# Windowed attention and a three-product MoE: queries, keys and values laid out by token and chunk, with an order of its own

## The chip, the cores and the metric

The kernel runs on one core of one Trainium2 chip. The metric is the device time of one execution in microseconds, the median of several; preparing the inputs on the host is not part of it. The engines are named as in the profile: PE is TensorE (PEld its weight loads), DVE VectorE, ACT ScalarE, POOL GpSimd, SP SyncE; SPq and ACTq are the two queues on which transfers are issued.

## The reference

Attention over 8 batches of 8 heads with 64 elements each: 512 local tokens look at the 32 global ones and at the local ones within 32 positions, and the 32 global tokens look at all 544. The 544 x 8 result rows of 512 elements (4352 rows) go through an MLP with a gate that is 0 below -1, h above 1 and a parabola between:

```python
k_all = np.concatenate([k_g, k_l], axis=2)
v_all = np.concatenate([v_g, v_l], axis=2)
out_g = np.matmul(sm(scale * np.matmul(q_g, k_all.transpose(0, 1, 3, 2))), v_all)
s_ll = np.where(np.abs(pos[:, None] - pos[None, :]) <= 32, scale * np.matmul(q_l, k_l.transpose(0, 1, 3, 2)), -1e9)
s_lg = scale * np.matmul(q_l, k_g.transpose(0, 1, 3, 2))
out_l = np.matmul(sm(np.concatenate([s_lg, s_ll], axis=-1)), v_all)
x = np.concatenate([out_g, out_l], axis=2).transpose(0, 2, 1, 3).reshape(B * S, H * D)
h = x @ w_in
g = np.where(h >= 1, h, np.where(h <= -1, 0.0, (h + 1) ** 2 / 4))
return (g @ w_out).astype(np.float32)
```

Queries, keys, values and the result are float32. The two weights, 512 x 2048 and 2048 x 512, come as float64, so 8 MB each.

## The kernel before, in words

Every number is carried as two float16 halves with a scale, and each product is made of three matrix products (high x high, high x low, low x high). The work is written as named steps.

**Weights.** 16 tiles of w_in (`load_win`, two transfers of 256 KB each, in rows of 1 KB) and 16 of w_out (two transfers of 256 KB, rows of 2 KB) are decoded from float64 words by integer operations, mostly on VectorE (`win_decode`, `wout_decode`), squared on TensorE for a scale, and split into halves.

**A batch.** `load` fetches queries, keys and values (lines 551 to 583). Tokens go to partitions, so a tile is 128 tokens x 8 heads x 64 elements. Queries: four tiles of 128 tokens and one of the 32 global ones. Keys and values: six tiles ("chunks"); the first five hold the 32 global tokens and 96 local ones, the last 32 global, 32 local and 32 global. In memory q_l is batch, head, token, element, so what one partition receives is eight pieces of 64 floats. A chunk takes two transfers (global and local part), the last one three: 13 transfers for the keys of a batch, 13 for the values, 5 for the queries. `scale_q`, `scale_k` and `scale_v` find a scale for each; for batch 0 the scales of queries and keys come from Gram products of the raw tiles on TensorE (`gram`, line 585; 24 products for the keys of six tiles), for the others from squares on ScalarE. `prep_q`, `prep_k` and `prep_v` split a tile in halves; queries and keys are then transposed, in batch 0 by TensorE with a copy from PSUM by ScalarE or VectorE, later by DMA transposes on SP's queue. `swap_q` and `prep_w` copy between on-chip tiles by transfers of 2 KB runs. `att_q` to `att_x` do the local attention, `glob_a` and `glob_b` the global one, `moe_f` and `moe2` the MLP of 256 tokens at a time (`moe1` for the first two).

**Order.** The steps are first recorded in order of a planned time and cut into segments (line 98), a run of calls on one engine; each transfer is a segment of its own. `ORDER` (line 1293) lists the segments' numbers in the order in which they are issued. TensorE, VectorE, ScalarE and GpSimd execute them exactly in that order; transfers are kept in the listed order within the queues that issue them, so a transfer on ScalarE's queue stands behind the ScalarE instructions ahead of it in the list. `SLOTS` gives each tile its place. `T["queues"]` says of each plain transfer whether SP's (s) or ScalarE's (a) queue issues it; a load on SP's queue waits until the load five before it there has landed (`AHEAD`, line 1342). Other letters of `T` choose the engine of an operation: `casts` and `subs` for the high and low half of the softmax, `turns` for the copy after a transposition, `glow`, `lows` and `lowx` for low halves in the MLP (v is VectorE, a ScalarE, p GpSimd). Since all instructions are replayed from one place, they have one line in the profile, L1365, plain transfers L1368 and DMA transposes L1370; groups are told apart by tiles.

Of the kernel before, what the change touches and what calls it, by code (L numbers as in the profile page):

```python
# [131 lines left out]
def attention_moe(nc, memory, q_l, k_l, v_l, q_g, k_g, v_g, w_in, w_out, out):  # L132
    B, H, S, D = q_l.shape
    SG = q_g.shape[2]
    DM, DFF = w_in.shape
    P = 128
# [4 lines left out]
    NTOK = SG + S  # L141
# [69 lines left out]
    def load_dma(o, i):  # L211
        nc.sync.load(o, i)
# [338 lines left out]
    def load_kv(src_l, src_g, b, nm, part):  # L551

        got = []
        for c in (2 * part, 2 * part + 1):
            if c == NC - 1:
                st = st4.tile([P, H, D], F32, tag="st4", name=f"{nm}{b}_{c}")
                for o in (0, 2 * QB):
                    load_dma(st[o:o + QB], src_g[b].rearrange("h p d -> p h d"))
                load_dma(st[QB:2 * QB], src_l[b][:, S - QB:S, :].rearrange("h p d -> p h d"))
                got.append((st, 3 * QB))  # L560
                continue
            st = stg.tile([P, H, D], F32, tag="st", name=f"{nm}{b}_{c}")
            load_dma(st[0:QB], src_g[b].rearrange("h p d -> p h d"))
            load_dma(st[QB:P], src_l[b][:, 96 * c:96 * c + 96, :].rearrange("h p d -> p h d"))
            got.append((st, P))
        return got

    def load_q(b, part):
        c = 2 * part
        if c == NI:  # L570
            st = st4.tile([P, H, D], F32, tag="st4", name=f"qg{b}")
            load_dma(st[0:SG], q_g[b].rearrange("h p d -> p h d"))
            return [(st, SG)]
        got = []
        for u in range(2):
            st = stg.tile([P, H, D], F32, tag="st", name=f"q{b}_{c + u}")
            load_dma(st, q_l[b][:, (c + u) * P:(c + u + 1) * P, :].rearrange("h p d -> p h d"))
            got.append((st, P))
        return got

    def load(b, nm, part):
        r = load_q(b, part) if nm == "q" else load_kv(*{"k": (k_l, k_g), "v": (v_l, v_g)}[nm], b, nm, part)
        BT[b].setdefault("raw" + nm, {}).update({2 * part + u: x for u, x in enumerate(r)})
# [710 lines left out]

SLOTS = {
# [49 lines left out]
def build(tc, *args):  # L1345
# [4 lines left out]
    with ExitStack() as ctx:  # L1350
# [10 lines left out]
        with tc.manual_schedule(engines={E.PE, E.DVE, E.Activation, E.Pool}):  # L1361
            for n in order:
                for engine, op, a, k in again[n]:
# [13 lines left out]
                    moved.append(r)  # L1377


_INS = ["q_l", "k_l", "v_l", "q_g", "k_g", "v_g", "moe_w_in", "moe_w_out"]  # L1380
_OUTS = [((4352, 512), "float32")]


# [23 lines left out]
```

## Time and profile before

| | |
|---|---|
| median of 3 runs | 893.72 us (892.99 to 897.49) |
| the profiled execution, its own time | 897.37 us |
| its span in the profile | 895.6 us |
| mean granted TensorE clock, of full speed | 0.991 |
| TensorE busy | 841.7 us (94%) |
| VectorE busy | 716.7 us (80%) |
| ScalarE busy | 645.8 us (72%) |
| GpSimd busy | 348.0 us (39%) |
| moved by transfers | 140.97 MB in 379,713 packets |

The span is from the first to the last instruction; the execution's own time has some 2 us around it. Busy shares are of the span, and say nothing of which engine a stage waits for; that is read from stretches and waits. The DMA share of a stretch can exceed 1.

### The profile page before, as it was taken

Reading aid. Unit: us, or ns where it says so; the run is one execution under the profiler, and the core shown is the slowest. Engines: PE = TensorE matmul, PEld = TensorE weight load, DVE = VectorE, ACT = ScalarE, POOL = GpSimd, SP = SyncE. Lnnn points to the kernel's source line nnn. Section 1 sums busy time; section 2 is a strip of 40 time slices with the busy share of each in tenths; the row PEclk is TensorE's granted clock in tenths of the full one; section 3 lists DMA queues with packets and bytes.
Section 4 is the critical chain, followed back from the end, with each engine's and each line's share of the span. In section 5 each row is a group of like instructions: output and inputs, shape, how many; then the busy total and the mean of one; then the engine's idle time right before and its main releaser. Section 6 shows DMA issues by size and latency. Waiting matters only on the chain.

```text
span 895.6 us, 35249 instructions
## 1 busy us (share of the span) xinstructions
PE 841.7 (94%) x14398; PEld 613.1 (68%) x14398; DVE 716.7 (80%) x1967; ACT 645.8 (72%) x1632; POOL 348.0 (39%) x545
## 2 busy tenths in 40 slices
PE   1667999999999999899999999999999999999998
PEld 1534899557876766867585967767676867588743
DVE  3998999997878997787878888788988988757741
ACT  2489998888787976785888767876888578455530
POOL 4236457725333244332346235323214233315160
PEclk9988999999999999999999999999999999999999
DMA  9998798599988999998997899999998974584001
GB/s 228 251 234 216 201 196 139 121 189 191 172 143 176 166 181 177 169 156 173 177 181 141 173 155 172 182 166 142 189 173 163 176 135 97 113 142 82 2 1 59
DMA packets 379713, 140.97 MB, mean 157 GB/s; under 512 B 348576, under 2 KB 357792, under 8 KB 379552
## 3 DMA queue, kind: packets, MB, share of 16 engines
q1 hardware_dynamic: 314864, 102.28, 66.6%
q10 hardware_dynamic: 64688, 36.45, 18.8%
q8 instruction: 112, 1.84, 0.9%
q14 instruction: 49, 0.40, 0.2%
HBM read 49.81 MB, written 8.91 MB: 66 GB/s over the span
## 4 chain that ended last, share of the span: by engine, by line
PE 69%; DMA 4%; DVE 4%; ACT 2%; issue 1%; SPq 0%; ACTq 0%; DVEq 0%
PE bank L1365 69%; DMA room<-room 3%; DVE room L1365 3%; ACT room L1365 2%; DMA keys_kt<-room 1%; DVE bank L1365 1%; DMA room<-in_v_g_dram 1%; ACTq L1368 0%; SPq L1368 0%; SPq L1370 0%; DVE weights_w L1365 0%; DVE small_nb L1365 0%; DVE batch_small_ms L1365 0%; DVE small_gs L1365 0%; DVE twin L1365 0%
## 5 line engine op out<-in xcount | busy, mean ns | idle before, releaser
L1365 POOL TENSOR_TENSOR room<-room,room 128x256 f16<-128x256 f32 (+4 forms) x408 | 278.5, 708 | 452.0 <-ACT room L1365 366.3
L1365 PEld LDWEIGHTS <-room 128*32 128x32 f16 (+3 forms) x7576 | 251.4, 97 | 235.9 <-issue 25.1
L1365 PE MATMUL bank<-weights_w,room 128*128 128x512 f16 x1632 | 366.4, 379 | 1.6 <-DVE room L1365 1.3
L1365 PEld LDWEIGHTS <-weights_w 128*128 128x128 f16 (+1 forms) x3968 | 220.2, 98 | 20.0 <-issue 6.8
L1365 PE MATMUL bank<-room,weights_w 128*128 128x128 f16 (+1 forms) x3840 | 220.4, 216 | 3.8 <-issue 3.0
L1365 ACT CAST room<-room 128x512 f16<-128x512 f32 (+1 forms) x245 | 140.1, 587 | 61.4 <-DVE room L1365 34.3
L1365 PE MATMUL bank<-room,twin 128*128 128x128 f16 (+1 forms) x2304 | 129.0, 216 | 0.5 <-ACT room L1365 0.5
L1365 PEld LDWEIGHTS <-twin 128*128 128x128 f16 x2304 | 123.6, 98 | 3.8 <-issue 0.6
L1365 ACT ACTIVATE room<-room,small_nb 128x128 f32<-128x128 f32 x256 | 100.8, 395 | 10.9 <-DVE small_nb L1365 9.0
L1365 ACT ACTIVATE room<-bank,batch_small_ms 128x512 f32<-128x512 f32 (+1 forms) x112 | 83.1, 750 | 31.9 <-DVE bank L1365 9.8
L1365 DVE SCALAR_TENSOR_TENSOR bank<-bank,batch_small_ms,room 128x512 f32<-128x512 f32 (+1 forms) x112 | 80.4, 723 | 12.6 <-ACT room L1365 12.4
L1365 ACT COPY room<-bank 128x512 f32<-128x512 f32 (+2 forms) x107 | 63.1, 596 | 33.0 <-PE bank L1365 18.0
L1365 ACT ACTIVATE junk_junka<-room 128x512 f16<-128x512 f32 (+2 forms) x120 | 74.9, 624 | 11.9 <-DMA room<-in_q_l_dram 3.1
L1365 DVE SCALAR_TENSOR_TENSOR room<-room,batch_small_ms,bank 128x512 f32<-128x512 f32 (+1 forms) x112 | 78.9, 711 | 1.2
L1365 DVE CUSTOM_DVE_ANT_0 room<-bank,const_mask,batch_small_q 128x128 f32<-128x128 f32 x256 | 73.7, 345 | 6.3 <-PE bank L1365 5.5
L1365 DVE TENSOR_TENSOR room<-room,room 128x512 f16<-128x512 f32 (+1 forms) x89 | 63.9, 724 | 17.5 <-ACT room L1365 16.4
L1365 DVE TENSOR_TENSOR bank<-bank,room 128x512 f32<-128x512 f32 (+1 forms) x64 | 41.5, 658 | 20.5 <-PE bank L1365 20.3
L1365 DVE SCALAR_TENSOR_TENSOR room<-room,batch_small_ms,room 128x512 f32<-128x512 f32 (+1 forms) x64 | 48.5, 760 | 3.0 <-ACT room L1365 2.6
L1365 DVE TENSOR_SCALAR room<-bank,batch_small_ms 128x512 f32<-128x512 f32 x34 | 25.1, 743 | 31.5 <-PE bank L1365 29.0
L1365 ACT ACTIVATION_READ_ACCUMULATOR room<-room,small_nb 128x1 f32 x256 | 48.8, 191 | 0.0
L1365 DVE SCALAR_TENSOR_TENSOR room<-room,batch_small_sv,room 128x512 f16<-128x512 f32 (+1 forms) x47 | 38.2, 818 | 5.6 <-ACT room L1365 5.1
L1365 DVE SCALAR_TENSOR_TENSOR room<-room,batch_small_sk,room 128x512 f16<-128x512 f32 (+1 forms) x46 | 35.7, 788 | 7.4 <-ACT room L1365 7.4
(174 smaller groups left out, 886.3 us busy)
## 6 DMA issues: line engine op xcount, KB each, us to landing
room<-room SPq DMA_DIRECT2D x75, 128.0 KB, 3.7
room<-room ACTq DMA_DIRECT2D x69, 128.0 KB, 3.7
twin<-in_moe_w_out_dram SPq DMA_DIRECT2D x22, 256.0 KB, 4.9
room<-in_q_l_dram SPq DMA_DIRECT2D x21, 256.0 KB, 5.1
room<-in_v_l_dram SPq DMA_DIRECT2D x28, 192.0 KB, 3.7
room<-in_k_l_dram SPq DMA_DIRECT2D x24, 192.0 KB, 4.2
weights_w<-in_moe_w_in_dram ACTq DMA_DIRECT2D x17, 256.0 KB, 4.5
out_dram<-room SPq DMA_DIRECT2D x17, 256.0 KB, 2.6
```

The source lines that it names most:

```text
L1365: getattr(getattr(tc.nc, engine), op)(*a, **k)
```

## The change

The host arranges the inputs: `q_all` is batch, token, head, element, local tokens first and then the global ones; `k_all` and `v_all` hold the six chunks of a batch one after another, 736 tokens, with the global tokens repeated in each chunk. A tile is then one transfer, 2 KB contiguous per partition. A batch's keys take 6 transfers instead of 13, its values 6 instead of 13, its queries 5 as before: 464 plain transfers in all instead of 576, with the same bytes.

```diff
-            if c == NC - 1:
-                st = st4.tile([P, H, D], F32, tag="st4", name=f"{nm}{b}_{c}")
-                for o in (0, 2 * QB):
-                    load_dma(st[o:o + QB], src_g[b].rearrange("h p d -> p h d"))
-                load_dma(st[QB:2 * QB], src_l[b][:, S - QB:S, :].rearrange("h p d -> p h d"))
-                got.append((st, 3 * QB))
-                continue
-            st = stg.tile([P, H, D], F32, tag="st", name=f"{nm}{b}_{c}")
-            load_dma(st[0:QB], src_g[b].rearrange("h p d -> p h d"))
-            load_dma(st[QB:P], src_l[b][:, 96 * c:96 * c + 96, :].rearrange("h p d -> p h d"))
-            got.append((st, P))
+            tail = c == NC - 1
+            n = 3 * QB if tail else P
+            st = (st4 if tail else stg).tile([P, H, D], F32, tag="st4" if tail else "st", name=f"{nm}{b}_{c}")
+            load_dma(st[:n], src[b, c * P:c * P + n])
+            got.append((st, n))
...
-            load_dma(st, q_l[b][:, (c + u) * P:(c + u + 1) * P, :].rearrange("h p d -> p h d"))
+            load_dma(st, q_all[b, (c + u) * P:(c + u + 1) * P])
...
+    def rows(*parts):
+        return _np.concatenate(parts, axis=2).transpose(0, 2, 1, 3)
+
+    def chunks(g, x):
+        return rows(*[y for c in range(0, 480, 96) for y in (g, x[:, :, c:c + 96])], g, x[:, :, 480:512], g)
+
+    laid["q_all"] = rows(inputs["q_l"], inputs["q_g"])
+    laid["k_all"] = chunks(inputs["k_g"], inputs["k_l"])
+    laid["v_all"] = chunks(inputs["v_g"], inputs["v_l"])
```

With it come a new `ORDER`, new `SLOTS`, new `queues` and new letters. Apart from the loads the segments are the same ones, so the old and the new list can be laid side by side. From the MLP chunks 8 and 9 on (batch 4; some 500 us into the execution before) the four engines' orders are the same as the old ones. Before that they differ:

- The old list begins with the query tiles 0 and 1 of batch 0, then mixes keys, the first weights and a part of the values; its last key transfer stands behind 11 half tiles of w_in. The new list begins on SP's queue with query tiles 2 and 3, the global queries, query tile 0, key chunk 4, query tile 1, key chunk 5, and then weights; on ScalarE's queue with key chunks 1, 2, 0 and 3, behind ScalarE's first instruction, the squares of the global queries, and then weights. No weights stand ahead of the last key chunk.
- Letters of batch 0 and of the first MLP chunk: one of `subs` goes from VectorE to GpSimd; in `casts` three go from VectorE to ScalarE and one the other way; in `turns` three go from VectorE to ScalarE (one of them a small copy) and two the other way; in `glow` two go from VectorE to GpSimd and one the other way; in `lows` one goes from GpSimd to VectorE. Later batches change in both directions.

## Rows read from the trace of the kernel before

**Rows 1.** The page: busy time of TensorE, then tenths of busy time in 40 slices.

```profile
PE 841.7 (94%) x14398; PEld 613.1 (68%) x14398; DVE 716.7 (80%) x1967; ACT 645.8 (72%) x1632; POOL 348.0 (39%) x545
...
PE   1667999999999999899999999999999999999998
...
DMA  9998798599988999998997899999998974584001
```

**Rows 2.** Stretches: us, busy us (instructions) by engine, granted TensorE clock, DMA share, GB/s.

```profile
0.00:30.00 30.00, 9.85 (x83) 7.74 (x84) 15.05 (x41) 8.68 (x13) 11.06 (x42) 1.00 1.13 230
30.00:112.00 82.00, 61.12 (x1068) 43.99 (x1068) 76.35 (x241) 69.92 (x177) 38.73 (x52) 0.92 0.94 224
112.00:500.00 388.00, 379.70 (x6590) 279.29 (x6588) 327.52 (x911) 314.26 (x808) 166.51 (x245) 1.00 0.96 167
500.00:860.00 360.00, 359.31 (x6517) 267.88 (x6516) 290.30 (x764) 249.51 (x628) 123.60 (x192) 1.00 0.80 137
```

**Rows 3.** What TensorE waited for, 0 to 112 us: total, times, longest.

```profile
PE bank L1365 <- DVE room L1365: 15.4, 7, 6.3
PE bank L1365 <- DMA room<-in_q_l_dram: 7.8, 4, 4.8
```

**Rows 4.** Timeline of VectorE, 0 to 50 us: start, us, instruction [idle before <-releaser].

```profile
6.42 0.30 DVE L1365 CUSTOM_DVE_ANT_0 bank<-bank,const_ident 128x128 f32<-128x128 f32 x1 [6.42 <-PE bank L1365]
...
11.15 0.30 DVE L1365 CUSTOM_DVE_ANT_0 bank<-bank,const_ident 128x128 f32<-128x128 f32 x1 [3.00 <-PE bank L1365]
...
16.40 0.43 DVE L1365 TENSOR_SCALAR room<-weights_w 128x512 f32<-128x512 f32 x1 [3.52 <-DMA weights_w<-in_moe_w_in_dram]
...
28.75 0.68 DVE L1365 SCALAR_TENSOR_TENSOR weights_w<-weights_w,bank 128x512 int32<-128x512 int32 x1
...
31.89 0.48 DVE L1365 TENSOR_SCALAR room<-room,batch_small_sk 128x512 f16<-128x512 f32 x1
```

**Rows 5.** Timeline of TensorE, 0 to 60 us.

```profile
26.68 1.44 PE L1365 MATMUL bank<-room 128*128 128x128 bf16 x12 [0.85 <-DMA room<-in_k_l_dram]
28.37 1.46 PE L1365 MATMUL bank<-room 128*128 128x128 bf16 x12 [0.25 <-DMA room<-in_k_g_dram]
```

**Rows 6.** Transfers of 0 to 30 us: packets by size.

```profile
DMA packets 15511, 6.90 MB, mean 230 GB/s; under 512 B 11592, under 2 KB 15447, under 8 KB 15511
```

**Rows 7.** Transfers of 11 to 13 us.

```profile
DMA packets 722, 0.69 MB, mean 347 GB/s; under 512 B 44, under 2 KB 722, under 8 KB 722
```

**Rows 8.** Transfers of 20 to 23 us.

```profile
DMA packets 2126, 0.52 MB, mean 174 GB/s; under 512 B 2126, under 2 KB 2126, under 8 KB 2126
```

**Rows 9.** The page: issues of transfers, KB each, median us from issue to landing.

```profile
room<-in_k_l_dram SPq DMA_DIRECT2D x24, 192.0 KB, 4.2
...
out_dram<-room SPq DMA_DIRECT2D x17, 256.0 KB, 2.6
```

**Rows 10.** Forms of VectorE, 0 to 200 us: busy us, mean ns.

```profile
L1365 DVE TENSOR_TENSOR room<-room,room 128x512 f16<-128x512 f32 x6 | 4.6, 770 | 0.0
...
L1365 DVE CAST room<-room 128x512 f16<-128x512 f32 x5 | 2.6, 514 | 0.2
```

**Rows 11.** Forms of ScalarE, 0 to 200 us.

```profile
L1365 ACT CAST room<-room 128x512 f16<-128x512 f32 x32 | 19.4, 620 | 4.0 <-POOL room L1365 2.1 <-DVE room L1365 0.7 <-DVE const_wo L1365 0.5
```

**Rows 12.** What TensorE waited for, 112 to 500 us.

```profile
PE bank L1365 <- issue: 3.1, 4, 1.4
PE bank L1365 <- DVE room L1365: 2.9, 5, 1.3
PE bank L1365 <- DMA room<-room: 1.6, 3, 0.7
```

**Rows 13.** The chain that ended last: start us, us, what.

```profile
340.81 4.11 DMA room<-room
344.94 5.56 DMA room<-room
```

**Rows 14.** The page: all packets of the execution, by size.

```profile
DMA packets 379713, 140.97 MB, mean 157 GB/s; under 512 B 348576, under 2 KB 357792, under 8 KB 379552
```

More of the change, by code (lines that the diff above doesn't have):

```diff
@@ L129, in plan, with attention_moe @@
     return order, sizes, taken
-def attention_moe(nc, memory, q_l, k_l, v_l, q_g, k_g, v_g, w_in, w_out, out):
-    B, H, S, D = q_l.shape
-    SG = q_g.shape[2]
+def attention_moe(nc, memory, q_all, k_all, v_all, w_in, w_out, out):
+    B, NTOK, H, D = q_all.shape
+    SG = 32
+    S = NTOK - SG
     DM, DFF = w_in.shape
@@ L140, in attention_moe @@
     NK = DM // P
-    NTOK = SG + S
     TAIL = NTOK - NI * P
@@ L549, in attention_moe, with load_kv @@
     BT = [dict() for _ in range(B)]
-    def load_kv(src_l, src_g, b, nm, part):
+    def load_kv(src, b, nm, part):
         got = []
         for c in (2 * part, 2 * part + 1):
-            if c == NC - 1:
-                st = st4.tile([P, H, D], F32, tag="st4", name=f"{nm}{b}_{c}")
-                for o in (0, 2 * QB):
-                    load_dma(st[o:o + QB], src_g[b].rearrange("h p d -> p h d"))
-                load_dma(st[QB:2 * QB], src_l[b][:, S - QB:S, :].rearrange("h p d -> p h d"))
-                got.append((st, 3 * QB))
-                continue
-            st = stg.tile([P, H, D], F32, tag="st", name=f"{nm}{b}_{c}")
-            load_dma(st[0:QB], src_g[b].rearrange("h p d -> p h d"))
-            load_dma(st[QB:P], src_l[b][:, 96 * c:96 * c + 96, :].rearrange("h p d -> p h d"))
-            got.append((st, P))
+            tail = c == NC - 1
[3 more added lines that the diff above has]
+            got.append((st, n))
         return got
@@ L571, in load_q @@
             st = st4.tile([P, H, D], F32, tag="st4", name=f"qg{b}")
-            load_dma(st[0:SG], q_g[b].rearrange("h p d -> p h d"))
+            load_dma(st[0:SG], q_all[b, S:NTOK])
             return [(st, SG)]
@@ L581, in load @@
     def load(b, nm, part):
-        r = load_q(b, part) if nm == "q" else load_kv(*{"k": (k_l, k_g), "v": (v_l, v_g)}[nm], b, nm, part)
+        r = load_q(b, part) if nm == "q" else load_kv(k_all if nm == "k" else v_all, b, nm, part)
         BT[b].setdefault("raw" + nm, {}).update({2 * part + u: x for u, x in enumerate(r)})
@@ L1326 @@
 T = dict(es="nnnn", gramq="paaaaaaa", dg="vvvvvvaaaaavvav", sid="vvvvv", fast=2, grams="ppaaaaaa", sqs="maamaa", cb=200, cbs=5, lk0=4.19,
-         lq0=1.76, lv0=12, sk=12, sq=14, subs="pvppppppvppppvvpvppppvvppppppppvpppppvpvpvppppppvvpvpvvppppvpvvv",
-         glow="pppppvpvppvppppppppvpppvvvppvpvpvppppvppppvppvvpvpvppppvppppvvpppppppppppvvvppppvppvvvvvvvpvppvpvvvpvppppvvppvvppppppvvpppvvpvpppppppppppppppppp",
-         turns="aaaavvaavvvavavaaaavaaa", casts="vavaavavaaavaaavaaavaaaavaavaaavavaaaaavavvavvvavavvavvvvvvaaaav",
-         mags="aapapvpaappvppppppapapaaaaapaaaa", lowx="ppppppvpppppvvpvvvpvpppvpvvvpvpvvpvvpppppvvvpvpp",
-         lows="ppppppppvpppvpppppppvpppvppppppp", halves="aaaaaahaabacadacceccacdbidffcbdf", shifts="vavvaaavvvvaaavvvvvavvvvvaaavvvv",
+         lq0=1.76, lv0=12, sk=12, sq=14, subs="ppppppppppvpvvpppppppppvvvppvvvvvvppvvpvpvppppppvvpvpvvppppvpvvv",
+         glow="ppppvpppppvppvpppppppvpvpvpvvvpppvppvpvvvpvpppvvvppppvpvppvpvpvvpppppppppvvvppppvppvvvvvvvpvppvpvvvpvppppvvppvvppppppvvpppvvpvpppppppppppppppppp",
+         turns="aaaaavaavaaavavavavvaaa", casts="aaaaavvaaaavvavavvavavaavavavvvaaavaaavvavvavvvavavvavvvvvvaaaav",
+         mags="aapapvpaappvppppppapapaaaaapaaaa", lowx="ppppppppppppppvvpppvpppvvvvvpvpvvpvvpppppvvvpvpp",
+         lows="pppvppppppvpppvpppppvpppvppppppp", halves="aaaaaahaabacadacceccacdbidffcbdf", shifts="vavvaaavvvvaaavvvvvavvvvvaaavvvv",
          splits="wpvpwwpvwwvpvvvw", att=1.35, s0=60, s1=100, s2=254.09, wd0=4, wds=2.06, wd8=19.2, wdt=1.9, wh=1.5, whs=1.4, od=58.2,
@@ L1334 @@
          sv=24.5, sqb=35.02, pk2=20.4, pk3=30, pk4=45.8, pq2=28.03, pq4=44, pv=35.24, pvs=0.33, lw=0.54, lo=32.46, los=2.12, mk=8, mks=2,
-         nbs="aavavaaaaaavaavvavvavavvvvvvavvavvavaavaavavvaaaaaavvvvavavavvva", dens="vaaavaavvavaavvvaavvvavvavvavaaa",
-         queues="ssaasaaasaaassssassaaaaassasaaaasassssaassaaaaaassssasssassassasssssassasasassssasssssssaaaasassssasaassassassssasssaaasssssaassassssssaasassaassasssaassassaasssssaaassaasssaaasaaasasasasassaasaasasssasasssaasasssaaasaassssssaaaaaasasaaasaaaaasassssaassssaassasaasasasssaasassssssaasasaaaaaaassssasssassaasaaasasssaasssssassssasssassaasssssasssaassssssssssaaaaassasasassssassssasasssassasssasassaasssssaasssassasaassassssasassssaasssssaaaasssaasassaasasssssassasassaaasaassssaaaaasssaasaasassaaasasaasaasssassssssaaasssssaasssassssasaassssasssasaassassasaaaasasaassaaasssaasss")
+         nbs="avvaaaaaaavvaavvvavvvvvvvavaavavvavaaavaavavvaaaaaavvvvavavavvva", dens="aavvaavaavaaavaaaavvvavvavvavaaa",
+         queues="asaaassassaaaasssaaaaaasssaasaaassssssssssaassssssassassssaassssssaassssasaasssasssassaassssaasasaaasssaasssassassassaaasssasaaasssssassaasaasasasasssaasssssssaaasaasssaasaassassaasssssssssasssaasasssssaasaasasssaaasasaasssaaassaassaasasasasssssssaasssssssaaaassassassasaaaaasaasassassssaaaassasasaasasasssasasasssaassaasssaaasaaassassssasassssaasssssaaaassaasasssssassasasaaassaaaasssaasaasassaaasasaasaasasssasssssaasssasssasasssasaassassasaaaasasaassaaasssaasss")
 KEYS = 2
@@ L1377, in build @@
                     moved.append(r)
-_INS = ["q_l", "k_l", "v_l", "q_g", "k_g", "v_g", "moe_w_in", "moe_w_out"]
+_INS = ["q_all", "k_all", "v_all", "moe_w_in", "moe_w_out"]
 _OUTS = [((4352, 512), "float32")]
@@ L1389 @@
     from concourse.bass_utils import run_bass_kernel_spmd as _run
+    def rows(*parts):
+        return _np.concatenate(parts, axis=2).transpose(0, 2, 1, 3)
+    def chunks(g, x):
+        return rows(*[y for c in range(0, 480, 96) for y in (g, x[:, :, c:c + 96])], g, x[:, :, 480:512], g)
+    laid = dict(inputs)
+    laid["q_all"] = rows(inputs["q_l"], inputs["q_g"])
+    laid["k_all"] = chunks(inputs["k_g"], inputs["k_l"])
+    laid["v_all"] = chunks(inputs["v_g"], inputs["v_l"])
     nc = _bacc.Bacc("TRN2", target_bir_lowering=False, num_devices=1)
@@ L1393 @@
     for name in _INS:
-        a = _np.ascontiguousarray(inputs[name])
+        a = _np.ascontiguousarray(laid[name])
         if a.dtype == _np.float64:
```

2 lines of the change are left out of this document (1 added, 1 removed), and 24 rows, old and new, of the table SLOTS.

## Prediction

> **What bounds the kernel now.** I read the busy shares first. TensorE is busy for 841.7 of 895.6 us, and in the tenths its only weak slices are the first four and the last two [rows 1]. The change adds and removes no matrix product, so the time can fall only by TensorE's idle time, 895.6 - 841.7 = 53.9 us.
>
> Where that lies is shown by the stretches [rows 2]. TensorE idles 20.2 us in the first 30 us, 20.9 us from 30 to 112, 8.3 us from 112 to 500, 0.7 us from 500 to 860; the rest is the tail. In the third and fourth stretch TensorE is busy 98% and more, so a faster load there has almost nothing to give. The case is decided in the first 112 us.
>
> What bounds those is read from VectorE's column. From 30 to 112 us VectorE is busy 76.35 of 82 us, ScalarE 69.92: decoding the weights, preparing keys and the first softmax leave VectorE no room, and TensorE waits for it (15.4 us of its idle time up to 112 us is put down to VectorE's tiles, 7.8 to query loads) [rows 2, 3]. In the first 30 us VectorE is busy 15.05 us and idle 14.95, while the DMA engines are never free [rows 2]. Its timeline shows the idle pieces: 6.42 us until the first query tile has come and been squared, 3.00 us for the second pair, 3.52 us for the first weights; the first product of the keys comes at 31.89 us, since the Gram products of the keys start at 26.68 and resume at 28.37, each time on a key transfer [rows 4, 5]. So the start is bound by transfers up to some 30 us, then by VectorE, then by TensorE.
>
> **The loads.** Each 2 KB token row of q, k and v now goes as eight runs of 256 B; it will go as one. Bytes stay the same. In the first 30 us, 11,592 packets are under 512 B, 2.97 MB of 6.90 [rows 6]. Two stretches price the sizes: with 1 KB rows of weights alone the engines move 347 GB/s, with 256 B rows alone 174 GB/s, the engines being full in both [rows 7, 8]. No stretch holds 2 KB rows alone; I take 347 GB/s from the nearest row, 1 KB. Then those 2.97 MB take 8.6 us instead of 17.1: **8.5 us** of transfer time is freed in the first 30 us. That is the upper end of the first term, since VectorE can win no more than the transfers do; the lower end is 0, if VectorE finds something else to wait for.
>
> The Trainium skill ("DMA: Bandwidth & Descriptors", section "Why small descriptors are slow (HBM only)") speaks against so much: it puts the loss of a 256-byte descriptor at about 3 cycles beside 8, 27%. By that the freed time would be at most 17.1 x 3/11 = 4.7 us (an estimate from that page), and the sum below some 3 us less. The factor of two between the two stretches is measured here, so it decides.
>
> What VectorE makes of it follows from the new order. Ahead of the last key tile now stand 11 half tiles of weights; in the new list all of batch 0's queries and keys go first, 1.11 + 1.51 = 2.62 MB, and no weights ahead of the last key on either queue but what slips in beside it. 2.62 MB at 347 GB/s are 7.6 us. The fixed part of a transfer: a 256 KB store with 2 KB rows lands 2.6 us after its issue, of which 0.76 is its bytes at 347 GB/s [rows 9], so 1.8 us. With the first issue near 1 us the last key would land at 10.4 us. Four key tiles stand on ScalarE's queue behind its first instruction, which waits for the global queries, the third transfer of the other queue, so I allow 1.6 us for a gap: **12 us**. From the first Gram product to the first product of the keys it takes 31.89 - 26.68 = 5.2 us now [rows 4, 5]; so that product comes at about **17 us**.
>
> VectorE's work ahead of it: of the 15.05 us of rows 2, twelve steps on weights, from 16.40 to 28.75 us, most of 0.42 to 0.69 us, make 7.8 us [rows 4]; so the query work is some 7.3 us. With the scale of the keys (about 1.3 us within the 5.2) and one weight step it is 9 us (an estimate). Idle until 17 us: 8 us; 1 us more for waits on the first weights, which flow when the keys are in, at 256 KB per 0.76 us against some 2 us of VectorE for a tile. So 9 us idle instead of 14.95: a gain of **6 us** (ends 0 and 8.5). It is passed on in full, as VectorE is the bound from there on [rows 2].
>
> **The letters.** For batch 0 and its first MoE chunk, VectorE gives up one subtraction (0.77 us), two casts (0.51 each), one small copy and, net, nothing among the low halves [rows 10]: 2.1 us. ScalarE takes the casts for 0.62 us each [rows 11] and GpSimd the subtraction; ScalarE has 12.1 us free between 30 and 112 [rows 2]. If ScalarE were late instead, 1.2 us would come back. I take **1.5 us** (ends 0 and 2.1).
>
> **Fewer transfers.** 112 of the 576 plain ones go, some from ScalarE's queue. They hide behind the engines' work once the start is over; the cover is that TensorE hardly idles there [rows 2]. Taken at 0. The doubled size of a key transfer also doubles what the pacing of five loads lets be under way on SP's queue; what is queued behind a waiting load there is the other DMAs of that queue, transposes among them. That cost is in the slow rival.
>
> **The middle.** From 112 to 500 us the order is new, after that every engine's order is the old one. TensorE's 8.3 us there wait for VectorE (2.9), transfers (1.6) and issue (3.1) [rows 12]. A new order with lighter transfers may save most of it or lose as much again; 0, with ends of 7 us either way.
>
> **Sum.** 6 + 1.5 = 7.5 us. The profiled execution took 897.4 us (span 895.6), 3.7 above the median of 893.72; it would take 889.9, and the median becomes **886.2 us**, 0.8% less. A measurement of this kernel can tell about 0.5%, 4.5 us, from no change; so faster means under 889.3, slower over 898.2.
>
> **Rivals.** *Hidden anyway* (893.7, between 889.3 and 898). The data comes sooner, but VectorE's idle time moves: weights now follow keys, and VectorE then waits for the first weight tiles or for the chain gram, scale, product, which no transfer shortens. For it: only 3.52 us of VectorE's idle time is put directly down to a transfer [rows 4]; 2 KB rows may move no faster than now from HBM, in which case the layout does not do what it is for. Against: the Gram products themselves waited for keys. Chance 0.23.
>
> *A larger gain* (880). If queries, keys and values of batch 1 are ready sooner too, VectorE's other 5.7 us of idle time before 112 us shrinks, and the middle gives 5 of its 8.3 us: 886.2 - 6 = 880. For it: the DMA engines are full almost to the end now [rows 1], and the chain contains two transfers between on-chip tiles of 4.11 and 5.56 us [rows 13] against the 2.6 us of rows 9. Against: TensorE waited only 1.6 us for them. Chance 0.20.
>
> *Slower* (900). A key or value load of 256 KB on SP's queue waits for a place or for the load five before it, and DMA transposes and swaps behind it go out late; keys of the next batch then miss their turn and TensorE, which executes in order, stops. Place: 112 to 500 us. Four batches are prepared there; a chain like that of rows 13, 9.7 us, uncovered twice gives 19.4 us, less the 7.5 won is 12 slower; uncovered once, 2 slower. It decides for "slower" when idle time there rises by over 12 us, from 8.3 to 20. For it: the chain already runs through such transfers. Against: TensorE has other work queued there. One and a half such chains give 900. Chance 0.09.
>
> **How the numbers follow.** Forecast (882.5 to 889.3) 0.48, larger gain 0.20, hidden 0.23, slower 0.09. Faster by over 0.5%: 0.48 + 0.20 = 0.68; within: 0.23; slower: 0.09. For 8 in 10 I leave out the slow rival and the far end of the larger gain: 886.2 less the 2 left of the first term, the letters' 0.6 and most of the middle's 7 is 878; the upper end is the hidden case's middle, 893.5.
>
> **What would show it.** Packets under 512 B fall from 348,576 [rows 14] by 129,024 (16,128 token rows of q, k and v, eight each). Right: VectorE's idle time in the first 30 us falls from 15 to about 9; the Gram products of the keys start near 12 us instead of 26.68 and their first product comes near 17 instead of 31.89; TensorE's idle time up to 112 us falls from 41 to some 33, that of 112 to 500 stays near 8. Wrong: VectorE's idle time in the first 30 us above 13 (hidden), TensorE's from 112 to 500 above 20 (slower) or under 4 (larger), or transfers of 2 KB rows below 300 GB/s with the engines full.

## The result, and the profile after

| | before | after |
|---|---|---|
| median, 4 runs each | 893.74 us (892.99 to 897.49) | 882.78 us (880.75 to 885.33) |
| profiled execution, its span | 897.37, 895.6 | 884.73, 883.0 |

The ratio is 0.9871, 95% interval [0.9827, 0.9914]: 11 us faster, where the forecast was 886.2 us (7.5 us). The two profiled executions differ by 12.6 us of span.

The page of the kernel after, its parts that answer to [rows 1, 14] (busy time of each engine; TensorE's tenths in 40 slices; packets by size):

```profile
PE 838.2 (95%) x14398; PEld 613.3 (69%) x14398; DVE 714.8 (81%) x1976; ACT 643.8 (73%) x1631; POOL 337.5 (38%) x529
...
PE   4678899999999999999989999999999999999998
...
DMA packets 265025, 140.97 MB, mean 160 GB/s; under 512 B 217760, under 2 KB 226976, under 8 KB 264864
```

The slices that were weak at the start (1, 6, 6, 7) are now 4, 6, 7, 8. Packets under 512 B fell by 130,816: the 129,024 of the forecast and 1,792 more, 16 for each of the 112 transfers that went.

The stretches of the kernel after, as in [rows 2] (us; busy us and instructions of TensorE, its weight loads, VectorE, ScalarE and GpSimd; granted clock, DMA share, GB/s):

```profile
0.00:30.00 30.00, 15.01 (x152) 12.47 (x153) 20.95 (x57) 16.84 (x27) 18.25 (x50) 0.86 0.87 278
30.00:112.00 82.00, 64.50 (x1282) 51.09 (x1281) 78.44 (x259) 76.21 (x189) 37.62 (x55) 0.95 0.95 247
112.00:500.00 388.00, 380.99 (x6560) 280.61 (x6558) 329.73 (x917) 306.61 (x796) 151.05 (x222) 1.00 0.85 166
500.00:860.00 360.00, 359.01 (x6331) 260.83 (x6329) 282.16 (x742) 244.16 (x621) 130.57 (x204) 1.00 0.69 130
```

Read it as length less busy time. TensorE's idle time up to 112 us is 15.0 + 17.5 = 32.5 us, where it was 41.0 (-8.5); from 112 to 500 it is 7.0 (8.3 before); the last stretch and the tail together are 0.7 us worse. That makes 9.1 us. The other 3.5 of the 12.6 is TensorE's own busy time, 838.2 instead of 841.7, of which the forecast had said nothing. A second profile of the same kernel (e5, below) has 32.2 us up to 112, 5.5 from 112 to 500 and 837.9 us busy: so idle times of one kernel can differ by 1.5 us from profile to profile. VectorE is idle for 9.05 us of the first 30, where it was 14.95.

The timelines of the kernel after at the start, one for each engine (start, us, instruction, idle time before and who ended it), beside [rows 4, 5]. VectorE:

```profile
5.16 0.30 DVE L1359 CUSTOM_DVE_ANT_0 bank<-bank,const_ident 128x128 f32<-128x128 f32 x1 [5.16 <-PE bank L1359]
...
17.37 0.53 DVE L1359 TENSOR_SCALAR room<-room,batch_small_sk 96x512 f16<-96x512 f32 x1
```

TensorE:

```profile
12.11 2.74 PE L1359 MATMUL bank<-room 128*128 128x128 bf16 x24 [0.21 <-DMA room<-in_k_all_dram]
```

ScalarE and its queue:

```profile
5.86 1.28 ACT L1359 ACT_TABLE_LOAD   x1 [5.86 <-DMA room<-in_q_all_dram]
5.95 1.35 ACTq L1362 DMA_DIRECT2D room<-in_k_all_dram  x3
...
7.34 0.44 ACTq L1362 DMA_DIRECT2D room<-in_k_all_dram  x1
```

The Gram products of the keys start at 12.11 us in one group of 24 (26.68 and 28.37 before, [rows 5]), and the first product of the keys at 17.37 (31.89). VectorE's first instruction comes at 5.16 us instead of 6.42. The gap that was allowed for ScalarE's queue is there to be seen: its first instruction, with the table load, waits until 5.86 us for the global queries, and the four key tiles leave behind it at 5.95 and 7.34. The Trainium skill ("ScalarE: Activation LUTs", section "What ACT_TABLE_LOAD costs") gives 1283 ns for that load; the row has 1.28 us.

### The profile page after: what moved, and what is told of

Same layout as the page of the kernel before. It is cut to its first block, busy times and chain, and to the rows that moved or that the text cites. A ratio compares the mean times of both kernels' runs of the same rounds, so it can differ in the third digit from the quotient of the medians.

```text
span 883.0 us, 35060 instructions
## 1 busy us (share of the span) xinstructions
PE 838.2 (95%) x14398; PEld 613.3 (69%) x14398; DVE 714.8 (81%) x1976; ACT 643.8 (73%) x1631; POOL 337.5 (38%) x529
## 4 chain that ended last, share of the span: by engine, by line
PE 77%; DMA 5%; DVE 5%; ACT 2%; issue 2%; POOL 1%; ACTq 0%; SPq 0%; DVEq 0%; POOLq 0%
PE bank L1359 77%; DMA room<-room 2%; DVE room L1359 2%; DMA keys_kt<-room 2%; ACT room L1359 2%; DVE bank L1359 1%; DMA room<-in_v_all_dram 1%; POOL room L1359 1%; ACT junk_junka L1359 1%; DVE weights_w L1359 1%; DMA room<-in_q_all_dram 0%; ACTq L1362 0%; DVE twin L1359 0%; SPq L1362 0%; DVE const_pgb L1359 0%
## 5 line engine op out<-in xcount | busy, mean ns | idle before, releaser
L1359 POOL TENSOR_TENSOR room<-room,room 128x256 f16<-128x256 f32 (+3 forms) x392 | 268.1, 710 | 458.1 <-ACT room L1359 312.0
L1359 ACT CAST room<-room 128x512 f16<-128x512 f32 (+1 forms) x240 | 136.9, 586 | 63.4 <-DVE room L1359 34.0
L1359 ACT ACTIVATE room<-room,small_nb 128x128 f32<-128x128 f32 x256 | 100.5, 394 | 12.6 <-DVE small_nb L1359 6.9
L1359 DVE SCALAR_TENSOR_TENSOR bank<-bank,batch_small_ms,room 128x512 f32<-128x512 f32 (+1 forms) x112 | 80.2, 722 | 17.6 <-ACT room L1359 17.5
L1359 DVE TENSOR_TENSOR room<-room,room 128x512 f16<-128x512 f32 (+1 forms) x97 | 70.3, 733 | 10.2 <-ACT room L1359 9.3
L1359 PE MATMUL bank<-keys_kt,room 128*32 128x128 f16 x2048 | 38.8, 225 | 10.9 <-DMA room<-room 6.0
L1359 DVE SCALAR_TENSOR_TENSOR room<-room,batch_small_sk,room 128x512 f16<-128x512 f32 (+1 forms) x46 | 37.8, 827 | 4.2 <-ACT room L1359 3.8
```

The lines of the kernel that those rows point to most:

```text
L1359: getattr(getattr(tc.nc, engine), op)(*a, **k)
```

## Experiments

Twelve kernels were run, one of them (e5) the changed kernel once more. Ratios are to the kernel before on the same chip, with the 95% interval; its medians there were 896.76 us (e1 to e4), 897.55 (e5 to e8) and 894.73 (e9 to e12). Three theories were on trial: that the transfers of the **start** carry the gain (A in the expectations, the forecast); that the **later batches** do (C); and that the **order and the letters** do, and the layout little (B). A fourth (D), that the number of transfers matters and not their rows, comes with e2. `SLOTS` and `queues` came with the order in every run; what they are worth alone wasn't tried.

**The layout alone, in the old order** (e1). A chunk's transfer is issued in the place of its first piece; everything else is the old list.

```diff
-                for o in (0, 2 * QB):
-                    load_dma(st[o:o + QB], src_g[b].rearrange("h p d -> p h d"))
-                load_dma(st[QB:2 * QB], src_l[b][:, S - QB:S, :].rearrange("h p d -> p h d"))
+                whole = (st[:3 * QB], src[b, c * P:c * P + 3 * QB])
+                for o in (0, 2 * QB, QB):
+                    load_dma(st[o:o + QB], src[b, c * P + o:c * P + o + QB], whole=whole, key=(nm, b, c))
...
+                    if "whole" in k:
+                        if k["key"] in done:
+                            continue
+                        done.add(k["key"])
+                        a = k["whole"]
...
```

> The kernel before with the new layout and one transfer per chunk, put where the first piece of the chunk stood in the old list; order of everything else, places and letters are the old ones. If the row length at the start makes the gain (A), the 8.5 us of transfer time freed in the first 30 us bring the Gram products of the keys from 26.7 to about 20 us, but 11 half tiles of weights still stand ahead of the keys, so VectorE's idle time in the first 30 us falls from 15 to about 11 and the time is 889 to 891. If the new order alone makes it (B), 893 to 894, as before. If the relief of the transfers all through the kernel makes it (C), 886 to 889, with TensorE's idle time from 112 to 500 us under 5 instead of 8.3.

0.9963 [0.9948, 0.9979]: 3.3 us by the ratio, of the 11. TensorE's timeline in e1:

```profile
22.40 2.74 PE L1365 MATMUL bank<-const_ident,room 128*128 128x128 f16 x24 [1.38 <-DVE room L1365]
24.93 1.63 PE L1365 MATMUL bank<-room 128*128 128x128 bf16 x24
```

The Gram products (24.93) no longer wait for a transfer: their row has no idle time. What holds them are the transposes ahead of them in the old list, which wait for VectorE (1.38 us in this row, 6.36 and 2.62 in two before it). The keys' first product comes at 30.67 us instead of 31.89. TensorE's idle time up to 112 us is 41.7 us, nothing less than before; from 112 to 500 it is 5.8, and its busy time is 839.6, so what e1 wins lies there and not at the start. So the rival "hidden anyway" is what happens when only the transfers change: the data is there, and an in-order engine doesn't come to it.

**The new order without the layout's two gains** (e2, e3, e4). e2 leaves the arrays head by head, so that a token row is eight runs of 256 B again, in one transfer a chunk. e3 keeps rows of 2 KB and splits each chunk into the old two (or three) transfers. e4 does both.

```diff
-        return _np.concatenate(parts, axis=2).transpose(0, 2, 1, 3)
+        return _np.concatenate(parts, axis=2)
...
+        if name in ("q_all", "k_all", "v_all"):
+            args[-1] = args[-1].rearrange("b h t d -> b t h d")
```

```diff
-            load_dma(st[:n], src[b, c * P:c * P + n])
+            load_pieces(st, src[b, c * P:c * P + n], (0, QB, 2 * QB, n) if tail else (0, QB, n))
...
```

> The changed kernel with the arrays held head by head in memory, so that each chunk is still one transfer, in the new order, but of 256 B runs. A: the 2.62 MB of queries and keys need 15 us instead of 7.6, the Gram products of the keys start near 19 us instead of 12.1, VectorE idles about 15 us in the first 30 instead of 9, and the time is 888 to 890. B: 882 to 884, as changed. D, that the number of transfers and their issue matters and not their rows: 882 to 884.

> The changed kernel with 2 KB rows, but each chunk of keys and values fetched in the old two transfers (three for the last chunk), one right behind the other on the same queue, each counted in the pacing of five. A: 882 to 884.5, since bytes and rows are the same and only the issue grows by 0.4 to 0.5 us for each. D: 887 to 891.

> Both undone: 256 B runs and the old number of transfers, with the new order, places and letters. A: 888 to 891, about as with 256 B runs alone. B: 882 to 885. D: 888 to 893, most of it in the number, so well above the run with 256 B runs alone.

| kernel | ratio | TensorE idle 0 to 112, 112 to 500 us | TensorE busy | VectorE idle 0 to 30, 30 to 112 |
|---|---|---|---|---|
| after (profiled 884.73) | 0.9871 [0.9827, 0.9914] | 32.5, 7.0 | 838.2 | 9.05, 3.56 |
| e2, 256 B rows | 1.0005 [0.9981, 1.0030] | 34.7, 15.3 | 843.4 | 11.2, 6.9 |
| e3, pieces | 1.0007 [0.9986, 1.0028] | 34.7, 13.3 | 841.8 | 11.9, 4.2 |
| e4, both | 1.0164 [1.0112, 1.0215] | 40.0, 22.3 | 846.5 | 13.4, 16.9 |

Either part undone takes the whole gain away, and both undone make the new list 1.6% slower than the old one. All three lie above every range that was expected of them. A quarter to a third of what each profile is longer than the one after (16.2, 11.2 and 32.8 us of span) is TensorE's busy time, not its idle time. No list was fitted anew to 256 B rows or to pieces, so these are prices in this list. The profiled executions of e2 and e4 were 4.6 and 7.8 us above their medians, so their idle times are up to that much too high. The stretch from 112 to 500 us of e3 (columns as above):

```profile
112.00:500.00 388.00, 374.67 (x6375) 274.92 (x6376) 324.77 (x900) 303.64 (x791) 152.08 (x224) 0.99 0.87 165
```

TensorE is busy 374.67 us there, against 380.99 after: 6.3 us of the loss (8.3 in e2) lie in a stretch where the forecast gave the transfers nothing.

The forecast's price for 256 B can be read from e2, where whole tiles come in such rows, and from e4, where they come in pieces. Transfers of 6 to 11 us in e2:

```profile
DMA packets 4265, 1.07 MB, mean 215 GB/s; under 512 B 4265, under 2 KB 4265, under 8 KB 4265
```

The same in e4:

```profile
DMA packets 3945, 0.98 MB, mean 197 GB/s; under 512 B 3945, under 2 KB 3945, under 8 KB 3945
```

With 2 KB rows, transfers of 6 to 12 us in the kernel after:

```profile
DMA packets 1381, 2.09 MB, mean 348 GB/s; under 512 B 129, under 2 KB 592, under 8 KB 1381
```

The same in e3:

```profile
DMA packets 898, 1.44 MB, mean 240 GB/s; under 512 B 185, under 2 KB 207, under 8 KB 898
```

With every packet of 256 B the engines move 215 GB/s, not the 174 of [rows 8], and 197 in pieces. So the keys' Gram products start sooner than expected, at 14.86 us in e2 (and 14.96 in e6, below). With 2 KB rows the engines move 348, as assumed from [rows 7], but 240 in pieces, and there they are not full (busy 0.82 of the time from 6 to 12 us, where it is 1.00 after). In the stretch after, three quarters of the bytes are in rows of 2 KB and the rest are weights in rows of 1 KB. The queues' timelines fit that. ScalarE's queue in e3, beside 1.35 + 0.44 us for four tiles above:

```profile
5.42 1.49 ACTq L1368 DMA_DIRECT2D room<-in_k_all_dram  x3
...
6.94 0.44 ACTq L1368 DMA_DIRECT2D room<-in_k_all_dram  x1
...
7.42 1.86 ACTq L1368 DMA_DIRECT2D room<-in_k_all_dram  x4
```

SP's queue in e3:

```profile
2.67 1.08 SPq L1368 DMA_DIRECT2D room<-in_k_all_dram  x2
...
8.71 1.24 SPq L1368 DMA_DIRECT2D room<-in_k_all_dram  x3
```

SP's queue in the kernel after, its last key tile:

```profile
5.87 0.33 SPq L1362 DMA_DIRECT2D room<-in_k_all_dram  x1
```

A queue needs 0.33 to 0.54 us to issue a transfer, a piece as much as a tile: eight pieces take 3.8 us where four tiles took 1.8. SP's last key pieces go out from 8.71 us on, the last key tile at 5.87; here it counts too that each piece takes a place in the pacing of five loads. And yet the keys are hardly later for it. TensorE in e3:

```profile
11.30 1.46 PE L1362 MATMUL bank<-room 128*128 128x128 bf16 x12
...
13.47 1.44 PE L1362 MATMUL bank<-room 128*128 128x128 bf16 x12 [0.70 <-DMA room<-in_k_all_dram]
```

VectorE in e3:

```profile
17.70 0.53 DVE L1362 TENSOR_SCALAR room<-room,batch_small_sk 96x512 f16<-96x512 f32 x1
...
26.64 0.70 DVE L1362 SCALAR_TENSOR_TENSOR bank<-bank,weights_w 128x512 int32<-128x512 int32 x1 [2.35 <-ACT weights_w L1362]
```

Half of the Gram products start at 11.30 us, before the 12.11 of the kernel after, the other half at 13.47, and both kernels are through with them at 14.9. The keys' first product comes at 17.70, where the two profiles of the changed kernel have 17.37 and 18.06 (e5). What VectorE idles longer in e3 lies behind ScalarE: 2.35 us for the weights at 26.64 (0.53 after) and 1.12 for the queries at 14.62 (none after).

**The changed kernel once more, and which batches carry it** (e5 to e7). e5 is the kernel after unchanged. e6 gives 256 B rows to batch 0 alone, e7 to batches 1 to 7 alone (`b > 0` in place of `b == 0`).

```diff
+    def by_token(src, b):
+        if not (b == 0):
+            return src[b]
+        return src[b].rearrange("t h d -> (t h d)").rearrange("(h t d) -> t h d", h=H, d=D)
...
-            load_dma(st[:n], src[b, c * P:c * P + n])
+            load_dma(st[:n], by_token(src, b)[c * P:c * P + n])
...
```

> The changed kernel as it is, beside the next three on the same chip, for a tighter ratio to the kernel before: 0.985 to 0.989.

> The changed kernel with 256 B runs for batch 0 alone (its tiles are stored head by head), 2 KB rows for the other seven. With 256 B runs for all, the loss was 11.4 us against the changed kernel: some 4 more us of TensorE idle time up to 112 us and 8 from 112 to 500. A, that the start carries it and the middle only inherits a late start: 6 to 9 us of the 11.4 here. C, that later batches carry it: 2 to 4 us here.

> The mirror of it: 2 KB rows for batch 0, 256 B runs for batches 1 to 7. A: 2 to 5 us lost against the changed kernel; C: 7 to 9, with TensorE's idle time from 112 to 500 us at 13 to 16 instead of 7. The two losses should add up to about 11.4.

e5 0.9851 [0.9810, 0.9893]; e6 0.9902 [0.9877, 0.9926]; e7 0.9942 [0.9917, 0.9967]. By medians batch 0 is worth 888.92 - 884.98 = 3.9 us and the later batches 894.10 - 884.98 = 9.1. The intervals of e5 and e6 overlap, though each run of e6 (887.59 and up) is above each of e5 (887.46 and down); those of e5 and e7 do not. Together they are 13.0 us, against 1.5% for e2. So by medians the rows of batch 0 carry some three tenths of what the long rows give in the new order. With 256 B rows in batch 0 the keys' Gram products still start at 14.96 us, and TensorE's idle time up to 112 us is 33.7. The keys are early even with all the old transfers, in TensorE's timeline of e4:

```profile
14.00 1.44 PE L1362 MATMUL bank<-room 128*128 128x128 bf16 x12 [0.65 <-DMA room<-in_k_all_dram]
...
16.28 1.44 PE L1362 MATMUL bank<-room 128*128 128x128 bf16 x12 [0.84 <-DMA room<-in_k_all_dram]
```

So the keys' sooner arrival is mostly the work of the new list, in which no weights stand ahead of the last key. The idle time isn't: in e4 it is 40.0 us up to 112.

What TensorE waited for from 112 to 500 us in e7 (total, times, longest):

```profile
PE bank L1364 <- issue: 10.0, 4, 3.4
...
PE bank L1364 <- DMA room<-room: 1.8, 3, 0.9
```

The same after:

```profile
PE bank L1359 <- issue: 3.5, 2, 1.9
PE bank L1359 <- DMA room<-room: 1.8, 3, 0.9
```

The waits that the profile puts down to a transfer are the same 1.8 us; "issue", time with no releaser in the profile, went from 3.5 to 10.0. (The profiled execution of e7 was 4.3 us above its median, so part of that is its own.) The page's issues of transfers (KB each, median us from issue to landing) do show the loads later. Keys on SP's queue in e7:

```profile
room<-in_k_all_dram SPq DMA_DIRECT2D x21, 256.0 KB, 5.0
```

And after:

```profile
room<-in_k_all_dram SPq DMA_DIRECT2D x21, 256.0 KB, 3.6
```

That the later landings are what makes TensorE late in e7 is argued from these rows, not shown link by link.

**Why pieces cost so much** (e8 to e10). In e3 each piece counts in the pacing of five loads; in e8 a chunk counts once. e9 splits only the chunks on SP's queue, e10 only those on ScalarE's.

```diff
+                    parts = [(a[0][x:y], a[1][x:y]) for x, y in zip(cuts, cuts[1:])] if cuts else [a]
+                    for a in parts:
...
+                        if op == "load" and queue[n] != "a" and len(loads) >= AHEAD:
+                            tc.add_manual_dep(r.ins, loads[-AHEAD].ins.name, paced, reason="paced")
+                        moved.append(r)
                     if op == "load" and queue[n] != "a":
-                        if len(loads) >= AHEAD:
-                            tc.add_manual_dep(r.ins, loads[-AHEAD].ins.name, paced, reason="paced")
                         loads.append(r)
```

e9 splits by queue (e10 has `"a"` in place of `"s"`):

```diff
+                    cuts = k.pop("cuts", None) if queue.get(n) == "s" else k.pop("cuts", None) and None
```

> Chunks fetched in pieces with 2 KB rows, as in the run that lost 11.6 us, but the pacing counts a chunk once, as in the changed kernel. If the doubled count is what made the pieces dear (the queue then runs ahead by half as many bytes), most comes back: 883 to 886 scaled to the kernel before at 894. If it is the issue of more transfers, on ScalarE's queue before anything else, it stays within 3 us of the pieces' time.

> The changed kernel with 2 KB rows, but the chunks that SP's queue fetches go in the old pieces (38 or so more transfers); those of ScalarE's queue stay whole. If the cost of the pieces is ScalarE's own time (each issue of 0.4 to 0.5 us on its queue stands between ScalarE's instructions, and ScalarE and VectorE set the pace up to 112 us), SP's pieces cost little: within 3 us of the changed kernel, ratio to the kernel before 0.985 to 0.989. If it is the number of transfers as such, about half of the loss of all pieces, 5 to 6 us, shows here.

> The mirror: only the chunks that ScalarE's queue fetches go in pieces (42 more transfers there, 19 us of issue at 0.45 us each). ScalarE's time: most of the 11.6 us is lost here, ratio 0.995 to 1.0. The number as such: about half, 0.991 to 0.994.

e8 1.0025 [0.9994, 1.0057]: the pacing is not the price. e9 0.9944 [0.9915, 0.9973], e10 0.9977 [0.9951, 1.0003]: either queue's pieces cost about 1% against the changed kernel (0.985 to 0.987), and both together 1.5%, so neither ScalarE's time nor one queue accounts for it. Nor is it the start: TensorE's idle time up to 112 us is 32.7 us in e9 and 32.4 in e10, as in the changed kernel. The rows above show how long the queues issue; how that makes the pieces dear, above all from 112 to 500 us, where e3 loses 6.3 us, stays open.

**The old letters in the new order** (e11). Eight strings (`subs`, `glow`, `turns`, `casts`, `lowx`, `lows`, `nbs`, `dens`) are those of before, for all batches; one is shown.

```diff
-         turns="aaaaavaavaaavavavavvaaa", ...
+         turns="aaaavvaavvvavavaaaavaaa", ...
```

> The changed kernel with the old choice of engines for subtractions, casts, copies and low halves (their places in the new order are kept). The forecast priced the letters of batch 0 at 1.5 to 2.1 us: 884 to 887 beside a kernel before of 894, ratio 0.988 to 0.992. If the new order depends on its letters throughout (a GpSimd subtraction of 0.74 us for each half, where VectorE takes 0.77 for the whole, comes late for the transposition behind it), more: 0.993 to 1.0.

1.0138 [1.0097, 1.0178], some 25 us above the changed kernel and above all that was expected. The stretch from 112 to 500 us of e11:

```profile
112.00:500.00 388.00, 365.79 (x6232) 266.59 (x6230) 314.89 (x864) 296.68 (x767) 167.26 (x239) 0.98 0.84 160
```

TensorE's waits there:

```profile
PE bank L1359 <- ACT room L1359: 6.3, 3, 3.0
PE bank L1359 <- DMA room<-room: 5.5, 6, 1.5
PE bank L1359 <- issue: 4.8, 3, 2.4
PE bank L1359 <- DVE room L1359: 4.1, 3, 3.4
```

TensorE idles 22.2 us, most of it over four causes of 4 to 6 us each, and GpSimd is busy 167.26 us instead of 151.05. In all, TensorE is also busy 848.3 us instead of 838.2. Up to 112 us it idles 30.7 us, less than the 32.5 after: the old letters cost no idle time at the start. The list depends on its letters through the middle. What the letters are worth in the old order, and those of batch 0 by themselves, wasn't tried.

**The keys earlier still** (e12). A tiny instruction takes ScalarE's table load at once, and the four key tiles are issued ahead of the squares.

```diff
-ORDER = ("290 174 175 3 285 286 2 217 291 292 ...
+ORDER = ("290 174 175 3 285 286 2 217 28 29 27 30 291 292 ...
...
+            tc.nc.gpsimd.memset(one, 0.0)
+            tc.nc.scalar.activation(two, one, AF.Exp)
...
```

> The changed kernel with ScalarE's start mended: its table is loaded by a tiny instruction that waits for no transfer, and the four key chunks on its queue are issued ahead of the squares of the global queries instead of behind them. The Gram products of the keys then start at 9.5 to 11 us instead of 12.1, unless the first query tiles, which now share the engines with them, come later by as much. VectorE sets the pace from there: a gain of 1 to 3 us, ratio 0.982 to 0.986, or none if the query chain becomes what the keys' scale waits for.

0.9890 [0.9856, 0.9924], no gain over the changed kernel. TensorE's timeline in e12:

```profile
4.19 0.61 PE L1363 MATMUL bank<-room 128*128 128x128 bf16 x4 [4.19 <-DMA room<-in_q_all_dram]
5.58 0.61 PE L1363 MATMUL bank<-room 128*128 128x128 bf16 x4 [0.78 <-DMA room<-in_q_all_dram]
...
8.45 0.61 PE L1363 MATMUL bank<-room 128*128 128x128 bf16 x4 [0.47 <-DMA room<-in_q_all_dram]
10.27 0.61 PE L1363 MATMUL bank<-room 128*128 128x128 bf16 x4 [1.21 <-DMA room<-in_q_all_dram]
...
12.52 2.74 PE L1363 MATMUL bank<-room 128*128 128x128 bf16 x24
```

The keys no longer make TensorE wait (12.52, with no idle time ahead), but each query tile does: 6.6 us in all, where it was 3.7. What the keys gained the queries lost, and the keys' first product comes at 17.84 us. No kernel tried beat the changed one.

## Why the prediction was right, and where its steps were not

- **The start.** Held in place and size: Gram products at 12 us (12.11), first key product at 17 (17.37), VectorE's idle time 9 us (9.05), TensorE's idle time up to 112 us 33 (32.5). The 347 GB/s held (348). What did not hold is the step from the loads to the term. It bounded VectorE's gain by the transfer time that long rows free, and read it off the keys' arrival. But the keys arrive some 12 us sooner with the new list and all the old transfers (e4: 14.00 and 16.28 us, before 26.68 and 28.37), and 1.8 sooner with the layout in the old list (24.93, e1); and VectorE then still idles 13.4 us (e4) and 13.6 us (e1) of the first 30. Either alone gives some 1.5 of the 5.9 us; the rest needs both.
- **The price of 256 B.** The step "those 2.97 MB take 8.6 us instead of 17.1" took 174 GB/s from a stretch in which 256 B rows came in pieces. Whole tiles of such rows moved 215 (e2), a factor of 1.6 instead of 2, and pieces 197 (e4); 2.97 MB at 215 GB/s are 13.8 us, so long rows alone free 5.2 us. The Trainium skill ("DMA: Bandwidth & Descriptors", section "Why small descriptors are slow (HBM only)") gave 27% for the first of two costs that it names; the measured 215 of 348 is 38% lost. The rate of 174 in [rows 8] was lower than that of e4's pieces; why, these runs don't say. The term of 6 us did not suffer, since it was built on the time of arrival.
- **Fewer transfers: 0.** Wrong. Putting the 112 transfers back into the new list costs 1.5% (e3). The step reasoned that TensorE hardly idles after the start, so nothing there could be lost; but small idle time can grow: from 112 to 500 us it is 13.3 us in e3 instead of 7.0. That transfers landing later do it is argued, not shown.
- **The middle: 0, ends of 7 us.** 1.3 us came, within its ends (2.8 in e5's profile); but the stretch is not indifferent to transfers, since 256 B rows in the later batches alone cost 9.1 us (e7). "A faster load there has almost nothing to give" is true of the old kernel and false of the new list, which needs the faster loads to stay at 7 us.
- **The letters: 1.5 us.** Not found where it was put. With all old letters in the new list TensorE idles no longer up to 112 us (30.7 us in e11, 32.5 after), so they are no separate saving at the start; they are a part of the list, and changing all of them back costs 25 us, 15 of them idle time from 112 to 500 us (e11).
- **TensorE's busy time, taken as fixed.** It fell by 3.5 us, and 2.6 of that is one group. The float32 products by form, before (count, busy us, mean ns, idle time ahead):

```profile
L1365 PE MATMUL bank<-weights_w,const_sid 128*128 128x512 f32 x26 | 16.1, 716 | 4.4 <-DVE const_sid L1365 3.6 <-ACT const_gpf L1365 0.8
```

And after:

```profile
L1359 PE MATMUL bank<-weights_w,const_sid 128*128 128x512 f32 x26 | 13.5, 632 | 2.7 <-DVE const_sid L1359 2.5 <-ACT room L1359 0.2
```

These are the same 26 products. A stretch of all engines before (columns as in the first table of stretches):

```profile
50.00:55.00 5.00, 2.69 (x33) 1.59 (x34) 4.80 (x23) 3.78 (x20) 2.12 (x4) 0.59 1.02 176
```

Stretches of TensorE before (us; busy us and instructions, granted clock, DMA share, GB/s):

```profile
78.00:80.00 2.00, 0.00 (x0) 1.00 0.73 182
...
86.00:88.00 2.00, 2.00 (x7) 0.50 0.90 227
```

Its float32 products in these:

```profile
54.11 2.08 PE L1365 MATMUL bank<-weights_w,const_sid 128*128 128x512 f32 x2 [0.74 <-DVE const_sid L1365]
...
86.31 2.02 PE L1365 MATMUL bank<-weights_w,const_sid 128*128 128x512 f32 x2
```

And after:

```profile
15.00:20.00 5.00, 2.67 (x24) 1.00 1.04 340
20.00:25.00 5.00, 2.54 (x23) 0.66 1.02 317
25.00:30.00 5.00, 4.03 (x56) 0.50 0.68 191
50.00:56.00 6.00, 4.89 (x12) 1.00 0.98 322
```

The first of these products after:

```profile
51.10 2.97 PE L1359 MATMUL bank<-weights_w,const_sid 128*128 128x512 f32 x6 [1.78 <-DVE const_sid L1359]
```

Before, the clock fell to 0.50 of full, the level of 1.2 GHz, in two places where these products stand: within the stretch from 50 to 55 us, and after TensorE had stood idle from 78 to 80 us. Two of them took 2.08 and two 2.02 us there, where six took 2.97 after (at 51.10). After, the low clock lies between 20 and 45 us, behind a stretch in which TensorE was busy 2.67 of 5 us, and at a time when it has small products and waits for VectorE anyway; from 50 us, where these products begin, the clock is 1.00. e5 has the same 13.5 us. In nine other kernels with the new list (e2 to e4, e6, e7, e9 to e12) the first six begin at 52 to 59 us, the clock falls to 0.50 while they run or has fallen before, and they take 4.6 to 5.3 us and the group 15.0 to 17.0. So 1.5 us and more of what each of those loses lies here. No run moved the low stretch by itself. TensorE's busy time is the largest part of what carried the result below 886.2: the forecast's 7.5 us, 1.0 more at the start, 1.3 in the middle and 3.5 here, less 0.7 at the end, make the 12.6 of the two profiled executions. That the total came so near is in part luck: 3.5 us came from a place that the forecast held fixed, and the 1.5 of the letters were not found at the start.

Of the **rivals**, "hidden anyway" describes the layout in the old order (e1), and the "slower" one, idle time from 112 to 500 us above 20, describes the new order without the layout (e4) or with the old letters (e11, 22.2). The forecast held because both came together. Its account of the shares did not hold: in the old order the layout gives 3.3 us, the new list with the old transfers takes 1.6%, and only the two together give 1.3 to 1.5%.

## What to carry to other kernels

Where in-order engines follow a fitted list, as here, faster transfers can pay little (0.4%) until the list is laid anew for them, and a list laid for them can be slower than the old one without them (1.6%): price the two together. A stretch in which the bound engine hardly idles shows that its loads come early enough, not that later loads would be free. In this list one transfer per tile counted for as much as long rows, though the keys came no later in pieces. And data that arrives sooner is not yet a gain: with the new list alone the keys came 12 us sooner, and the kernel was slower.

## What was not expected of the hardware

- Splitting tiles of 2 KB rows into transfers of 32 and 96 rows took the rate from 348 to 240 GB/s between 6 and 12 us (after, e3): the engines were then not full (0.82), and the queues' issue is the likeliest limit. The keys' first product was no later for it than in e5 (17.70 and 18.06 us).
- 256 B rows moved 215 GB/s in whole tiles, 197 in pieces, at full engines in both (a DMA share of 1.35 from 6 to 11 us).
- Each transfer adds 16 packets under 512 B: 112 fewer transfers took 1,792 away, and splitting 52 (e9) and 60 (e10) brought 832 and 960 back.
- The same 26 float32 products took 16.1 us in one list and 13.5 in another, by where the granted clock was 0.50.
